# A fused convolution and feed-forward kernel: block 0 of x loaded by POOL ahead of the weights, first weight quarter cast by ScalarE

## The chip, the core and the metric

The kernel runs on one core of one Trainium2 chip. Its engines work side by side, each with an instruction queue of its own: TensorE (PE, with weight loads shown as PEld), VectorE (DVE), ScalarE (ACT), GpSimd (POOL) and SyncE (SP). They meet through semaphores. DMA transfers are issued from the queues of SP, ACT and POOL and carried by 16 DMA engines. A transfer that changes the type (fp32 in DRAM to bf16 on chip) is issued by POOL in this kernel. SBUF has 128 partitions; PSUM takes the matmul results.

The metric is the device time of one execution in microseconds, the median of the runs.

## The reference, cut to what matters

```python
# x (8, 3904, 192), weight (8, 7); moe_w1, moe_w2 (192, 1024); moe_w3 (1024, 1024); moe_w_out (1024, 192)
w = softmax(weight, axis=-1)                     # 7 taps for each of 8 heads of 24 channels
x_pad = concat([zeros(B, 6, 192), x], axis=1)    # each sequence starts with zeros
attn[b, s, h, g] = sum_k w[h, k] * x_pad[b, s + k, h, g]
t = attn.reshape(31232, 192)
out = ((t @ w1) * (t @ w2) @ w3) @ w_out         # (31232, 192), fp32
```

The second line of matrices is linear after the product, so the kernel computes W = w3 @ w_out once, and then `(a * b) @ W`.

## The kernel before, in words

The 31232 tokens are cut into two halves of 15616 tokens, `r = 0` and `r = 1`. Half 0 stands on partitions 0 to 63 and half 1 on 64 to 127 wherever 64 rows of a contraction are enough, so that two matmuls with 64 rows each run on the array together. The weights `w1` and `w2` are the tiles `wd[0]` and `wd[1]`, `[128, 3, 1024]` in bf16; each holds its weight twice, once on each half of the partitions.

**Convolution.** A window is 64 rows of x, of which 58 give outputs. A block is a number of windows (`SIZES` is 10, 8, 10, 34, ...), loaded as `xb`. For each head a 64x64 band matrix in `Aband` holds the 7 taps, and a matmul (line 271) of band and window gives the convolved rows, which are moved to `convo`. The bands are made in four steps of `band(g, e, f)`: VectorE multiplies taps and diagonals (line 230, `cprod`), TensorE sums 14 matmuls (line 236), and the engine `f` moves the result to `Aband` (line 238). For the first blocks TensorE transposes `convo` (line 324) and the result is moved to `xT`; later blocks are stored to DRAM (`rows`, line 315) and come back by transposing DMAs (line 344).

**First product.** `first_product(R)` goes through 8 feature blocks of 128 columns (`ft`) for 512 tokens of each half. For each `ft` there are 12 matmuls for `w1` and 12 for `w2` (line 371, written together as `wd`), ScalarE copies the one result (line 377, `asb`), and VectorE multiplies it with the other (line 378, `abT`). `between` puts other work after the feature block with the given number. PSUM is given out as four pairs of banks in rotation.

**Second product.** `second_product` (line 397) multiplies `abT` with `W_sb`, ScalarE moves the result (line 402), and a DMA stores it. W itself is made once after the first three rounds: TensorE transposes w3 (line 433) and multiplies it with w_out (line 443).

**The order.** It is written out by hand: instructions stand in each engine's queue in the order of the program. Within the prologue it is this:

- SP loads block 0 of x in fp32 into `x32`, which takes a buffer of the `abT` ring: six transfers (lines 153 to 158).
- POOL makes `diag` (two `affine_select`, line 169), then copies two values of `x32` into `pace`, so that its queue waits for x (line 173), and then issues the weight loads, which cast to bf16 (line 166). They come in quarters of 256 columns (`WC`): quarter 0 of `wd[0]` and `wd[1]` to partitions 0 to 63, quarter 0 of `wd[0]` once more to partitions 64 to 127, and then quarters 1, 2 and 3 of both to partitions 0 to 63.
- SP copies what is missing on partitions 64 to 127 from partitions 0 to 63 by DMA, seven transfers (`copy_w`, line 350).
- ScalarE casts the first half of block 0 (line 201) and three windows of the second (line 462); VectorE casts the last two (line 467) and zeroes the six rows ahead of the sequence's start in half 1 (line 465).
- TensorE runs four matmuls on zeros, the broadcast of the taps, two more on zeros (line 187, `warm`), the bands, the convolution and the transposes of block 0, and then `first_product(0)`. The convolution of block 1 stands after its feature block 5, with the second half's results moved by VectorE, and its transposes after feature block 6.
- After the weights POOL issues the loads of blocks 1 and 2, then w_out, the eight row blocks of w3, and blocks 3 and 4 (`load_wo`, `load_w3`, `load_x`).

Of the kernel before, what the change touches and what calls it, by code (L numbers as in the profile page):

```python
# [8 lines left out]
FP32 = mybir.dt.float32  # L9
# [7 lines left out]
def kernel(  # L17
# [39 lines left out]
    def tok(i):  # L57
        return (i // WB) * S + (i % WB) * ST
# [3 lines left out]
    work = ctx.enter_context(tc.tile_pool(name="work", bufs=2))  # L62
# [8 lines left out]
    def banks():  # L71
        p = free.pop(0)
        return p, pairs[:, NS * p:NS * p + NS, :]
# [14 lines left out]
    def halves_of(b):  # L88
        n = SIZES[b] // 2
        return [(FIRST[b], 2 * n)] if 2 * n <= MAXN else [(FIRST[b], n), (FIRST[b] + n, n)]  # L90

    x_rows = x.rearrange("b s d -> (b s) d")
    xb_of, zero_rows = {}, {}

    def x_spans(r, i, m):
        return bass.AP(tensor=x.tensor, offset=(r * TS + tok(i) - PAD) * D,
                       ap=[[D, Q], [ST * D, m], [1, D]])

    def load_x(b, parts=(0, 1)):
        tiles = xb_of.setdefault(b, [])  # L100
        zeros_of = zero_rows.setdefault(b, [])
        for i0, n in [v for e, v in enumerate(halves_of(b)) if e in parts]:
            xb = work.tile([128, n, D], BF16, tag="xb", bufs=5, name="xb")
            w = 0
            while w < n:
                i = i0 + w
                m = min(n - w, WB - i % WB)
                at_end = i + m == NWIN
                if at_end:
                    m -= 1  # L110
                if m:
                    for r in range(NS):
                        nc.gpsimd.dma_start(out=xb[Q * r:Q * r + Q, w:w + m, :],  # L113
                                            in_=x_spans(r, i, m))
                if i % WB == 0:
                    zeros_of += [(xb, 0, w), (xb, 1, w)]
                w += m
                if at_end:
                    nc.gpsimd.memset(xb[Q:128, w, :], 0.0)
                    t = tok(NWIN - 1) - PAD  # L120
                    nc.gpsimd.dma_start(out=xb[0:Q, w, :], in_=x_rows[t:t + Q, :])
                    nc.gpsimd.dma_start(out=xb[Q:Q + PAD + LAST, w, :],
                                        in_=x_rows[TS + t:TS + t + PAD + LAST, :])
                    w += 1
            if len(halves_of(b)) == 1:
                tiles += [(xb, 0), (xb, SIZES[b] // 2)]
            else:
                tiles.append((xb, 0))
# [4 lines left out]
    n0 = SIZES[0] // 2  # L133
    xb0 = work.tile([128, 2 * n0, D], BF16, tag="xb", bufs=5, name="xb")
    xb_of[0] = [(xb0, 0), (xb0, n0)]
    x32 = work.tile([128, 2 * n0, D], FP32, tag="abT", bufs=GROUP, name="x32")
    pace = const.tile([1, 2], BF16)
    tiny = const.tile([128, 1], FP32)
    ones = const.tile([128, 1], BF16)
# [4 lines left out]
    nc.vector.memset(tiny, 0.0)  # L144
    nc.vector.memset(ones, 1.0)
    nc.vector.memset(zeros, 0.0)  # L146
    nc.vector.memset(x32[0:Q, 0, :], 0.0)
    nc.vector.memset(half, 0.0)
    nc.vector.memset(half[:, Q:2 * Q], 1.0)
    nc.vector.memset(identw, 0.0)  # L150
    nc.scalar.activation(out=tiny, in_=tiny, func=ACT.Exp)

    nc.sync.dma_start(out=x32[Q:128, 0:n0, :], in_=x_spans(1, 0, n0))
    nc.sync.dma_start(out=x32[0:Q, 1:n0, :], in_=x_spans(0, 1, n0 - 1))
    for s0, s1 in ((PAD, PAD + 48), (PAD + 48, Q)):
        nc.sync.dma_start(out=x32[s0:s1, 0, :], in_=x_rows[s0 - PAD:s1 - PAD, :])
    for r in range(NS):
        nc.sync.dma_start(out=x32[Q * r:Q * r + Q, n0:, :], in_=x_spans(r, n0, n0))

    WC = (0, DFF // 4, DFF // 2, DFF * 3 // 4, DFF)  # L160
    wd = [const.tile([128, NP, DFF], BF16, name=f"wd{i}", tag=f"wd{i}") for i in range(2)]
    w_rows = [w.rearrange("(k q) f -> q k f", q=Q) for w in (moe_w1, moe_w2)]

    def load_w(part, i, r=0):
        cs = slice(WC[part], WC[part + 1])
        nc.gpsimd.dma_start(out=wd[i][Q * r:Q * r + Q, :, cs], in_=w_rows[i][:, :, cs])  # L166

    for p0 in (0, Q):
        nc.gpsimd.affine_select(
            out=diag[p0:p0 + Q], in_=ones[p0:p0 + Q].to_broadcast([Q, Q + PAD]),  # L170
            pattern=[[-1, Q + PAD]], compare_op=ALU.is_equal, fill=0.0, base=0,
            channel_multiplier=1)
    nc.gpsimd.tensor_copy(out=pace, in_=x32[0:1, n0 - 1, 0:2])
    load_w(0, 0)
    load_w(0, 1)
    load_w(0, 0, 1)
    for part in range(1, len(WC) - 1):
        for i in range(2):
            load_w(part, i)
    ident, swapped = identw[:, 0:128], identw[:, Q:Q + 128]  # L180

    def warm(n, t=None):
        p = None
        if t is None:
            p, t = banks()
# [12 lines left out]
    nc.vector.tensor_tensor(  # L198
        out=wall, in0=wall, in1=wmax.unsqueeze(2).to_broadcast([1, H, K]), op=ALU.subtract)
    nc.scalar.activation(out=wall, in_=wall, func=ACT.Exp)  # L200
    nc.scalar.copy(out=xb0[:, 0:n0, :], in_=x32[:, 0:n0, :])
    nc.vector.tensor_copy(out=identw[0:Q, 0:Q], in_=diag[0:Q, 0:Q])
    nc.vector.tensor_copy(out=identw[0:Q, 128:128 + Q], in_=diag[0:Q, 0:Q])
    nc.vector.reduce_sum(out=wsum, in_=wall, axis=AX.X)
# [2 lines left out]
        out=wrow, in0=wall, in1=wsum.unsqueeze(2).to_broadcast([1, H, K]), op=ALU.mult)  # L207
# [20 lines left out]
    def band(g, e, f):  # L228
        c = slot([128, K, Q], BF16, "cprod")
        nc.vector.tensor_tensor(  # L230
            out=c, in0=taps, in1=wsb[:, g, e].unsqueeze(2).to_broadcast([128, K, Q]),
            op=ALU.mult)
        p, bps = banks()
        for v, lhsT in enumerate((ident, swapped)):
            for k in range(K):
                nc.tensor.matmul(bps[:, 0, v * Q:v * Q + Q], lhsT, c[:, k, :],
                                 start=(k == 0), stop=(k == K - 1))
        f(out=Aband[:, g, e].rearrange("p v s -> p (v s)"), in_=bps[:, 0, 0:2 * Q])
        drained(p)
# [78 lines left out]
    def pe_transpose(b, k):  # L318
        n = SIZES[b] // 2
        convo = convo_of[b]  # L320
        p, tps = banks()
        tps = bf16(tps)
        for w in range(n):
            nc.tensor.transpose(
                out=tps[:, w, :],
                in_=convo[:, w, k].rearrange("p r g -> p (r g)"), identity=ident)
# [21 lines left out]
    def copy_w(part, i, f):  # L348
        cs = slice(WC[part], WC[part + 1])
        f(out=wd[i][Q:128, :, cs], in_=wd[i][0:Q, :, cs])  # L350
# [70 lines left out]
    def load_wo():  # L421
        nc.gpsimd.dma_start(out=wo_b, in_=wor)
# [26 lines left out]
    V, A, P = nc.vector.tensor_copy, nc.scalar.copy, nc.gpsimd.tensor_copy  # L449

    def move(f, pair):
        f(out=pair[0], in_=pair[1])

    copy_w(0, 1, nc.sync.dma_start)
    for part in range(1, len(WC) - 1):
        for i in range(2):
            copy_w(part, i, nc.sync.dma_start)
    load_x(1)
    load_x(2)

    band(0, 0, A)
    A(out=xb0[:, n0:n0 + 3, :], in_=x32[:, n0:n0 + 3, :])
    band(0, 1, A)
    band(1, 0, A)
    nc.vector.memset(xb0[Q:Q + PAD, 0, :], 0.0)
    band(1, 1, A)
    V(out=xb0[:, n0 + 3:, :], in_=x32[:, n0 + 3:, :])
    for h, f in ((0, V), (2, A), (4, V), (6, A)):
        p, moves = conv(0, h, 2, ())
        for m in moves:  # L470
# [2 lines left out]
    for k, f in ((0, V), (1, A), (2, V)):  # L473
        p, *m = pe_transpose(0, k)
        move(f, m)
        drained(p)
    load_wo()
    for jt in range(JT):
        load_w3(jt)
# [3 lines left out]
    def seq(*fs):  # L483
        def run():
            for f, *a in fs:
                f(*a)
        return run

    first_product(0, {
        5: seq((conv, 1, 0, 4), (conv, 1, 4, 4, (V,))),  # L490
        6: seq((pe_transposes, 1))})
    first_product(1, {
        0: seq((conv, 2, 0, 4)),
# [80 lines left out]
```

## Time and profile before

| what | value |
|---|---|
| median of 3 runs | 531.38 us (530.8 to 532.62) |
| the profiled execution's own time | 532.29 us |
| its span on the core | 530.5 us |
| mean granted TensorE clock | 0.993 |
| TensorE busy | 519.4 us, 98% of the span |
| VectorE, ScalarE busy | 361.8 us (68%), 325.6 us (61%) |
| POOL busy | 55.5 us (10%) |
| share of the chain that ended last | TensorE 86% |

The span is the time from the first to the last instruction of the profiled execution; its own time, measured from outside, is 1.79 us longer. Rows of the timeline begin with start and duration in microseconds; in brackets stands how long the engine was idle before, and what ended that. Rows of groups end with busy time and mean duration in ns, and after the second bar with the idle time before them. Rows that begin with two times and a colon are stretches of the span: for each engine the busy time and the number of instructions, then the granted clock, the DMA engines' share and GB/s.

### The profile page before, as it was taken

Reading aid. Unit: us, or ns where it says so; the run is one execution under the profiler, and the core shown is the slowest. Engines: PE = TensorE matmul, PEld = TensorE weight load, DVE = VectorE, ACT = ScalarE, POOL = GpSimd, SP = SyncE. Lnnn points to the kernel's source line nnn. Section 1 sums busy time; section 2 is a strip of 40 time slices with the busy share of each in tenths; the row PEclk is TensorE's granted clock in tenths of the full one; section 3 lists DMA queues with packets and bytes.
Section 4 is the critical chain, followed back from the end, with each engine's and each line's share of the span. In section 5 each row is a group of like instructions: output and inputs, shape, how many; then the busy total and the mean of one; then the engine's idle time right before and its main releaser. Section 6 shows DMA issues by size and latency. Waiting matters only on the chain.

```text
span 530.5 us, 12833 instructions
## 1 busy us (share of the span) xinstructions
PE 519.4 (98%) x5482; PEld 346.1 (65%) x5482; DVE 361.8 (68%) x349; ACT 325.6 (61%) x410; POOL 55.5 (10%) x95
## 2 busy tenths in 40 slices
PE   6899999999999999999999999999999999999997
PEld 4345786557955579555894558845588555995587
DVE  5478664996559964699537994389943999038940
ACT  4488726775367743777437774377733777357752
POOL 6451024110002100021000200012000000000000
PEclk9799999999999999999999999999999999999999
DMA  7999299992478933788356964569445411430014
GB/s 128 198 201 190 38 205 188 184 144 66 147 178 119 111 90 124 177 117 107 90 151 160 123 90 114 147 153 120 62 120 161 118 32 31 135 122 1 1 61 150
DMA packets 128749, 64.39 MB, mean 121 GB/s; under 512 B 82168, under 2 KB 126839, under 8 KB 128691
## 3 DMA queue, kind: packets, MB, share of 16 engines
q1 hardware_dynamic: 89153, 43.29, 32.9%
q0 software_dynamic: 39392, 20.18, 29.3%
q8 instruction: 43, 0.70, 0.6%
q14 instruction: 15, 0.12, 0.1%
q10 hardware_dynamic: 146, 0.10, 0.1%
HBM read 33.45 MB, written 34.82 MB: 129 GB/s over the span
## 4 chain that ended last, share of the span: by engine, by line
PE 86%; DVE 1%; ACT 0%; issue 0%; POOL 0%; ACTq 0%; POOLq 0%
PE pairs L371 53%; PE pairs L397 31%; PE pairs L271 2%; DVE abT L378 1%; PE pairs L443 1%; ACT asb L377 0%; PE pairs L433 0%; ACT osb L402 0%; POOL pace L532 0%; ACTq L402 0%; POOLq L532 0%
## 5 line engine op out<-in xcount | busy, mean ns | idle before, releaser
L378 DVE TENSOR_TENSOR abT<-asb,pairs 128x1024 bf16<-128x1024 bf16 (+1 forms) x248 | 298.3, 1204 | 85.6 <-ACT asb L377 40.3
L371 PE MATMUL pairs<-xT,wd 64*128 64x512 bf16 (+1 forms) x2976 | 322.7, 375 | 3.9 <-DMA wd<-wd 2.8
L377 ACT CAST asb<-pairs 128x1024 bf16<-128x1024 f32 (+1 forms) x248 | 247.6, 998 | 75.7 <-PE pairs L371 75.3
L371 PEld LDWEIGHTS <-wd 64*128 64x128 bf16 x2976 | 164.8, 94 | 157.3 <-issue 7.5
L397 PEld LDWEIGHTS <-abT 128*128 128x128 bf16 x1952 | 159.8, 98 | 9.0 <-issue 9.0
L397 PE MATMUL pairs<-W_sb,abT 128*128 128x192 bf16 x1952 | 165.6, 246 | 0.0
L402 ACT COPY osb<-pairs 128x384 f32<-128x384 f32 x122 | 58.3, 478 | 117.0 <-PE pairs L397 117.0
L288 DVE CAST convo<-pairs 128x864 bf16<-128x864 f32 (+8 forms) x67 | 52.6, 840 | 56.6 <-PE pairs L271 56.6
L113 POOL DMA_DIRECT2D xb<-in_x_dram x38 | 30.1, 801 | 10.3 <-PE pairs L371 3.4
L532 POOL COPY pace<-abT 1x2 bf16<-1x2 bf16 x10 | 1.8, 177 | 251.7 <-DVE abT L378 251.7
L271 PE MATMUL pairs<-xb,Aband 64*64 64x432 bf16 (+4 forms) x320 | 16.7, 307 | 0.5 <-DVE abT L378 0.2
L402 DVE COPY osb<-pairs 128x192 f32<-128x192 f32 x1 | 0.4, 358 | 16.4 <-PE pairs L397 16.4
L271 PEld LDWEIGHTS <-Aband 64*64 64x64 bf16 x320 | 6.5, 105 | 6.0 <-issue 4.1
L409 POOL DMA_DIRECT2D out_dram<-osb x6 | 4.6, 771 | 25.5 <-ACT osb L402 25.5
L288 ACT CAST convo<-pairs 128x816 bf16<-128x816 f32 (+6 forms) x11 | 6.3, 614 | 1.0 <-PE pairs L271 1.0
L443 PE MATMUL pairs<-wo_b,w3T 128*128 128x192 bf16 x64 | 6.3, 246 | 0.1
L443 PEld LDWEIGHTS <-w3T 128*128 128x128 bf16 x64 | 5.2, 97 | 1.5 <-issue 1.5
L166 POOL DMA_DIRECT2D wd<-in_moe_w_dram x9 | 5.8, 653 | 0.0
L426 POOL DMA_DIRECT2D w3b<-in_moe_w_dram x8 | 4.3, 552 | 6.2 <-DMA xb<-in_x_dram 5.3
L433 PE MATMUL pairs<-identw,w3b 128*128 128x128 bf16 x64 | 4.6, 219 | 0.0
L436 DVE COPY w3T<-pairs 128x1024 bf16<-128x1024 bf16 x4 | 2.8, 690 | 2.4 <-ACT W_sb L445 1.4
L187 PE MATMUL pairs<-zeros 128*128 128x512 bf16 x6 | 2.9, 625 | 1.3 <-DVE zeros L146 1.3
(54 smaller groups left out, 49.0 us busy)
## 6 DMA issues: line engine op xcount, KB each, us to landing
out_dram<-osb SPq DMA_DIRECT2D x54, 384.0 KB, 3.6
xb<-in_x_dram POOLq DMA_DIRECT2D x14, 432.0 KB, 7.4
rows<-convo SPq DMA_DIRECT2D x6, 648.0 KB, 7.9
out_dram<-osb POOLq DMA_DIRECT2D x6, 384.0 KB, 9.3
w3b<-in_moe_w_dram POOLq DMA_DIRECT2D x8, 256.0 KB, 11.4
xb<-in_x_dram POOLq DMA_DIRECT2D x4, 408.0 KB, 12.9
xb<-in_x_dram POOLq DMA_DIRECT2D x4, 384.0 KB, 6.6
xT<-rows SPq DMA_TRANSPOSE x84, 3.0
```

Of the source, the lines that this page charges most:

```text
L113: nc.gpsimd.dma_start(out=xb[Q * r:Q * r + Q, w:w + m, :], in_=x_spans(r, i, m))
L166: nc.gpsimd.dma_start(out=wd[i][Q * r:Q * r + Q, :, cs], in_=w_rows[i][:, :, cs])
L271: nc.tensor.matmul(view(slice(Q * c, Q * c + Q), r)[:, :, j * G:(j + 1) * G], band_of(h, r), xb[Q * r:Q * r + Q, w0:w0 + n, h * G:(h + 1) ...
L288: f[e % len(f)](out=dst, in_=part)
L371: nc.tensor.matmul(p[:, r, 0:N], wd[i][rs, k, ft * 128:(ft + 1) * 128], xT[k][rs, r0:r0 + N], start=(k == 0), stop=(k == NP - 1))
L377: nc.scalar.copy(out=asb[:, :, 0:N], in_=pa[:, :, 0:N])
L378: nc.vector.tensor_tensor(out=ab[:, ft, :, 0:N], in0=asb[:, :, 0:N], in1=pb[:, :, 0:N], op=ALU.mult)
L397: nc.tensor.matmul(ops[:, (g - g0) * D:(g - g0) * D + D], ab[:, jt, r, g * 128:(g + 1) * 128], W_sb[:, jt, :], start=(jt == 0), stop=(jt = ...
L402: f(out=osb[:, g0:g0 + per, :].rearrange("p g d -> p (g d)"), in_=ops[:, 0:per * D])
L409: queue.dma_start(out=out[t0:t0 + ng * 128, :].rearrange("(g p) d -> p g d", p=128), in_=osb)
L433: nc.tensor.transpose(out=tps[:, gt, :], in_=w3b[:, gt * 128:(gt + 1) * 128], identity=ident)
L443: nc.tensor.matmul(wps[:, 0, 0:D], w3T[:, gt, :], wo_b[:, gt, :], start=(gt == 0), stop=(gt == JT - 1))
```

## The change

Block 0 of x no longer passes through fp32 on chip: POOL loads it into `xb0` with the cast in the DMA, in four transfers (nine windows for each half, and the 58 rows of the first window for each half), of which the first stands ahead of the `affine_select`s; there is no `pace` copy any more in the prologue. The rows ahead of the sequences' starts are zeroed by VectorE at the start. SP loads quarter 0 of both weights as fp32 into `wfirst`, and ScalarE casts each to both halves (`cast_w`). The other quarters are loaded by POOL, quarter 3 behind block 1 of x, and copied to partitions 64 to 127 by VectorE (quarter 1) and POOL (quarters 2 and 3). The last band is moved by VectorE; two matmuls on zeros stand behind the bands. Half of block 1's convolution moves from feature block 5 to 3, and ScalarE moves all its results.

```diff
-    x32 = work.tile([128, 2 * n0, D], FP32, tag="abT", bufs=GROUP, name="x32")
+    wfirst = work.tile([Q, 2, NP, DFF // 4], FP32, tag="abT", bufs=GROUP, name="wfirst")
...
-    nc.vector.memset(x32[0:Q, 0, :], 0.0)
+    nc.vector.memset(xb0[:, 0, :], 0.0)
...
-    nc.sync.dma_start(out=x32[Q:128, 0:n0, :], in_=x_spans(1, 0, n0))
-    nc.sync.dma_start(out=x32[0:Q, 1:n0, :], in_=x_spans(0, 1, n0 - 1))
-    for s0, s1 in ((PAD, PAD + 48), (PAD + 48, Q)):
-        nc.sync.dma_start(out=x32[s0:s1, 0, :], in_=x_rows[s0 - PAD:s1 - PAD, :])
-    for r in range(NS):
-        nc.sync.dma_start(out=x32[Q * r:Q * r + Q, n0:, :], in_=x_spans(r, n0, n0))
...
+    for i in range(2):
+        nc.sync.dma_start(out=wfirst[:, i], in_=w_rows[i][:, :, 0:WC[1]])
+
+    def load_w(part):
         cs = slice(WC[part], WC[part + 1])
-        nc.gpsimd.dma_start(out=wd[i][Q * r:Q * r + Q, :, cs], in_=w_rows[i][:, :, cs])
-
+        for i in range(2):
+            nc.gpsimd.dma_start(out=wd[i][0:Q, :, cs], in_=w_rows[i][:, :, cs])
+
+    def load_x0(r):
+        nc.gpsimd.dma_start(out=xb0[Q * r:Q * r + Q, 1:, :], in_=x_spans(r, 1, 2 * n0 - 1))
+
+    load_x0(0)
     for p0 in (0, Q):
         nc.gpsimd.affine_select(
...
-    nc.gpsimd.tensor_copy(out=pace, in_=x32[0:1, n0 - 1, 0:2])
-    load_w(0, 0)
-    load_w(0, 1)
-    load_w(0, 0, 1)
-    for part in range(1, len(WC) - 1):
-        for i in range(2):
-            load_w(part, i)
+    load_x0(1)
+    for r in range(NS):
+        nc.gpsimd.dma_start(out=xb0[Q * r + PAD:Q * r + Q, 0, :],
+                            in_=x_rows[r * TS:r * TS + ST, :])
+    load_w(1)
+    load_w(2)
+    load_x(1)
+    load_w(3)
+    load_x(2)
...
-    nc.scalar.copy(out=xb0[:, 0:n0, :], in_=x32[:, 0:n0, :])
...
-    copy_w(0, 1, nc.sync.dma_start)
-    for part in range(1, len(WC) - 1):
-        for i in range(2):
-            copy_w(part, i, nc.sync.dma_start)
-    load_x(1)
-    load_x(2)
-
+    def cast_w(i, r):
+        A(out=wd[i][Q * r:Q * r + Q, :, 0:WC[1]], in_=wfirst[:, i])
+
+    cast_w(0, 0)
+    cast_w(0, 1)
+    cast_w(1, 0)
     band(0, 0, A)
-    A(out=xb0[:, n0:n0 + 3, :], in_=x32[:, n0:n0 + 3, :])
     band(0, 1, A)
     band(1, 0, A)
-    nc.vector.memset(xb0[Q:Q + PAD, 0, :], 0.0)
-    band(1, 1, A)
-    V(out=xb0[:, n0 + 3:, :], in_=x32[:, n0 + 3:, :])
+    band(1, 1, V)
+    cast_w(1, 1)
+    warm(2)
...
+    for part, f in ((1, V), (2, P), (3, P)):
+        for i in range(2):
+            copy_w(part, i, f)
     load_wo()
...
     first_product(0, {
-        5: seq((conv, 1, 0, 4), (conv, 1, 4, 4, (V,))),
+        3: seq((conv, 1, 0, 4)),
+        5: seq((conv, 1, 4, 4)),
         6: seq((pe_transposes, 1))})
```

`V`, `A` and `P` are the copies of VectorE, ScalarE and POOL.

More of the change, by code (lines that the diff above doesn't have):

```diff
@@ L162 @@
     w_rows = [w.rearrange("(k q) f -> q k f", q=Q) for w in (moe_w1, moe_w2)]
-    def load_w(part, i, r=0):
+    for i in range(2):
+        nc.sync.dma_start(out=wfirst[:, i], in_=w_rows[i][:, :, 0:WC[1]])
+    def load_w(part):
         cs = slice(WC[part], WC[part + 1])
-        nc.gpsimd.dma_start(out=wd[i][Q * r:Q * r + Q, :, cs], in_=w_rows[i][:, :, cs])
+        for i in range(2):
[3 more added lines that the diff above has]
+    load_x0(0)
     for p0 in (0, Q):
```

## The prediction

> **What bounds the kernel now.** I read the page first, then the timeline of the first 16 us, then stretches of 2 us with the granted clock, then the waits. The page:
>
> ```profile
> span 530.5 us, 12833 instructions
> PE 519.4 (98%) x5482; PEld 346.1 (65%) x5482; DVE 361.8 (68%) x349; ACT 325.6 (61%) x410; POOL 55.5 (10%) x95
> L371 PE MATMUL pairs<-xT,wd 64*128 64x512 bf16 (+1 forms) x2976 | 322.7, 375 | 3.9 <-DMA wd<-wd 2.8
> ```
>
> TensorE is busy for 98% of the span. Line 371, the first product, is idle 3.9 us in 2976 matmuls, and 2.8 of that is one wait for a copy of the weights inside SBUF. So nearly everything after the prologue is TensorE's own work, and a microsecond taken from its start comes off the end. The timeline of TensorE shows where the wait lies:
>
> ```profile
> 8.28 0.57 PE L236 MATMUL pairs<-cprod,identw 128*128 128x64 bf16 x14 [0.99 <-DVE cprod L230]
> 8.78 1.03 PE L271 MATMUL pairs<-xb,Aband 64*64 64x120 bf16 x32
> 10.21 1.12 PE L324 MATMUL pairs<-identw,convo 128*128 128x128 bf16 x15 [0.40 <-ACT convo L452]
> 11.26 1.32 PE L371 MATMUL pairs<-xT,wd 64*128 64x512 bf16 x7
> 15.42 1.04 PE L371 MATMUL pairs<-xT,wd 64*128 64x512 bf16 x4 [2.84 <-DMA wd<-wd]
> ```
>
> The product starts at 11.26, stops after 7 matmuls and goes on at 15.42. It also goes on slowly. In the next rows (stretches of 2 us; then stretches with line 371 alone) the figure behind the busy times is the granted clock:
>
> ```profile
> 14.00:16.00 2.00, 0.58 (x4) 0.29 (x6) 0.00 (x0) 0.00 (x0) 2.00 (x3) 0.65 1.33 188
> 20.00:22.00 2.00, 2.00 (x14) 0.78 (x12) 0.89 (x2) 1.01 (x1) 0.03 (x1) 0.65 1.36 213
> 15.40:21.40 6.00, 5.98 (x30) 2.16 (x32) 0.50 1.41 195
> 21.40:25.40 4.00, 4.00 (x39) 1.79 (x35) 1.00 1.43 205
> ```
>
> From 15.4 to 21.4 the clock is 0.50: 30 matmuls in 6 us, then 39 in 4. A mean of 0.65 in 14 to 16 and again in 20 to 22 puts the half clock from about 14.6 to 21.4. Half of the 6.0 us that were worked in it, 3.0 us, is lost. So the late weights cost 2.84 in waiting and 3.0 in clock, 5.84 us.
>
> Why they are late:
>
> ```profile
> 5.96 0.18 POOL L173 CAST pace<-x 1x2 bf16<-1x2 f32 x1 [4.36 <-DMA x<-in_x_dram]
> 6.08 5.81 POOL L166 DMA_DIRECT2D wd<-in_moe_w_dram  x9
> 10.06 7.24 SPq L350 DMA_DIRECT2D wd<-wd  x7
> SPq L350 <- DMA wd<-in_moe_w_dram: 7.1, 3, 5.4
> DMA to landing us min/median/max: 6.7/6.7/6.7
> ```
>
> POOL holds the weights back until x has landed (5.96), then issues nine transfers. SP waits for one to land before it can copy it to the other half (10.06), and that copy of `wd[1]`, in a queue full of other weights, takes 6.7 us (last row, line 350): the chain x, weights, copy is serial.
>
> **The change part by part.**
>
> *First quarter of weights.* SP issues two fp32 loads at once in place of six x loads; ScalarE casts each to both halves, four casts of 64x768. The copy by DMA and its 6.7 us are gone. Rows for the casts and for the loads:
>
> ```profile
> 0.82 0.76 SPq L153 DMA_DIRECT2D x<-in_x_dram  x1
> L201 ACT CAST xb<-x 128x960 bf16<-128x960 f32 x1 | 1.0, 992 | 3.4 <-DMA x<-in_x_dram 3.4
> L462 ACT CAST xb<-x 128x576 bf16<-128x576 f32 x1 | 0.7, 674 | 0.7 <-DMA x<-in_x_dram 0.7
> 0.00:2.00 2.00, 0.67 (x2) 0.28 (x3) 0.89 (x7) 0.64 (x1) 0.69 (x6) 1.00 0.00 0
> 4.00:6.00 2.00, 2.00 (x24) 1.27 (x24) 1.87 (x4) 0.00 (x0) 0.04 (x1) 1.00 0.89 196
> 8.00:10.00 2.00, 1.53 (x46) 1.12 (x45) 1.18 (x4) 1.65 (x6) 2.00 (x4) 1.00 1.08 133
> ```
>
> From 992 and 674 ns, a cast costs 0.83 ns an element and 0.19 us: 0.83 us for 768, 3.3 us for four. The two ScalarE casts of x, 1.67 us, go away. The weights are 2 x 196 KB; at 196 GB/s (the row of 4 to 6 us, fp32 loads) they take 2.0 us alone. SP's first issue stands at 0.82 and nothing moves before 2 us (0 GB/s in the row of 0 to 2); from about 2.2, shared with x, they land at about 4.5 and 5.5. ScalarE then casts from 4.5: three done at about 7.0, three band evictions of 0.27 until 7.8, the fourth at 8.6. The product needs it at 11. Cost on the path: nothing, with 2.4 us of cover; beyond that, microsecond for microsecond.
>
> *x of block 0.* Two transfers of nine windows and two of single rows, now by POOL with the cast in the DMA, two `affine_select`s between them. Rows:
>
> ```profile
> 1.06 0.54 POOL L169 TENSOR_SCALAR_AFFINE_SELECT diag<-ones 64x70 bf16<-64x70 bf16 x2 [0.53 <-DVE ones L145]
> L113 POOL DMA_DIRECT2D xb<-in_x_dram x38 | 30.1, 801 | 10.3 <-PE pairs L371 3.4 <-DMA w3b<-in_moe_w_dram 3.2 <-DMA xb<-in_x_dram 2.8
> L121 POOL DMA_DIRECT2D xb<-in_x_dram x1 | 0.6, 561 | 0.0
> 8.29 0.67 ACT L462 CAST xb<-x 128x576 bf16<-128x576 f32 x1 [0.75 <-DMA x<-in_x_dram]
> DMA  9999999899997963200000005479999978899899
> 2.46 0.16 DVE L202 COPY identw<-diag 64x64 bf16<-64x64 bf16 x1
> ```
>
> POOL issues from about 0.8: 0.80 + 0.54 + 0.80 + 2 x 0.56, all out by 4.1. Data: 0.49 MB as bf16 at 133 (cast loads, 8 to 10 us) to 196 GB/s is 2.5 to 3.7 us, and the first weights 2.0 beside it, so 4.5 to 5.7 us from 2.2: the last packet at 6.7 to 7.9, and 0.9 to land: the row of digits is the DMA engines' busy share from 6 to 9 us in 40 slices, and x's last packets end in its 19th, at 7.4, where ScalarE is released at 8.29. I take 8.0. Bounds: 6.8 if the two streams overlap fully; 10.3 if x takes what the fp32 x took (8.29) and the weights' 2.0 come on top. `diag` moves from 1.6 to about 2.2; VectorE copies it at 2.46 today, so that is covered by 0.3 us, and costs what it exceeds.
>
> The Trainium skill ("DMA: Bandwidth & Descriptors", Why a DMA increments its semaphore by 16 and not by 1) has the number of engines of a transfer as the largest divisor up to 16 of its slowest dimension, with an exception for some transfers by GpSimd: 58 rows would go over 2 engines, and this stands against the new row loads. No run here shows it; the sum doesn't use it.
>
> *Bands.* Today VectorE's zeroing waits for ScalarE's cast of x, and holds up the fourth product:
>
> ```profile
> 4.21 1.70 DVE L230 TENSOR_TENSOR cprod<-diag,wsb 128x448 bf16<-128x448 bf16 x3
> 4.89 2.40 PE L236 MATMUL pairs<-cprod,identw 128*128 128x64 bf16 x42
> 7.45 0.14 DVE L465 MEMSET xb<- 6x96 uint32 x1 [1.54 <-ACT xb L201]
> 7.60 0.62 DVE L230 TENSOR_TENSOR cprod<-diag,wsb 128x448 bf16<-128x448 bf16 x1
> L238 ACT CAST Aband<-pairs 128x128 bf16<-128x128 f32 x4 | 0.9, 266 | 0.0
> ```
>
> The zeroing moves to the start, so the fourth product follows at 5.9 and its matmuls run on from 7.29 to about 7.9 (0.57 to 0.8 us). Two added warming matmuls wait for a bank that ScalarE drains behind its casts, at about 7.3; they take 0.4 to 1.0, to 8.4 to 8.9. The convolution starts at about 8.5 (today 8.78), bound below by 8.2, above by x at 10.3. From there to the product it is 11.26 - 8.78 = 2.48, so the product starts at 11.0: 0.3 us gained, between 0.6 gained and 1.6 lost.
>
> *The other quarters.* SP's remaining copies go to VectorE (quarter 1) and POOL (2 and 3). One feature block of the product takes 2.60 us (41.62 / 16):
>
> ```profile
> 83.95 41.62 PE L371 MATMUL pairs<-xT,wd 64*128 64x512 bf16 x384
> L378 DVE TENSOR_TENSOR abT<-asb,pairs 128x1024 bf16<-128x1024 bf16 x24 | 29.3, 1221 | 12.8 <-PE pairs L371 7.6 <-ACT asb L377 3.9
> L377 ACT CAST asb<-pairs 128x1024 bf16<-128x1024 f32 x24 | 24.3, 1014 | 13.0 <-PE pairs L371 13.0
> L452 DVE COPY xT<-pairs 128x580 bf16<-128x580 bf16 x2 | 0.9, 460 | 0.2 <-PE pairs L324 0.2
> L119 POOL MEMSET xb<- 64x192 bf16 x1 | 0.3, 258 | 0.0
> 53.79 1.54 PE L433 MATMUL pairs<-identw,w3b 128*128 128x128 bf16 x24
> ```
>
> So the quarters are needed at 11.0, 16.2, 21.8 (with a convolution half between) and 27.5. POOL issues quarter 1 by 5.4 and quarter 2 by 6.7; with x ahead in the queue they land at about 9.5 and 11. VectorE's two copies (460 ns for 580 elements, so at most 0.6 each) come at about 11.8, ahead of its first multiplication, which waits for matmuls until 13.6: covered. POOL's copies have no row; the nearest is a 64x192 memset of 258 ns, so 0.26 to 1.03 us for four times the elements; I take 1.0, and four of them, done by about 16 once quarter 3 has landed at 14. That is 5 us or more ahead of need. POOL then issues w_out and the w3 rows at about 16, not 14.67, into emptier DMA engines (0.67 MB of copies are gone); w3 is first used at 53.79 today, about 48 afterwards. Nothing.
>
> *Convolution of block 1* starts at feature block 3, with evictions by ScalarE alone. Its x is issued by 8 and needed at 21. Zero to 0.3; I take 0.1, since ScalarE's own copy of a block takes 1.01 of each 2.60 us there.
>
> *Sum.* 2.84 + 3.0 + 0.3 - 0.1 = 6.0 off 530.5: span 524.5. The profiled execution took 532.29, 1.79 more than its span, and 0.91 more than the median 531.38. Against the median: 525.4.
>
> **The rivals.**
>
> *The clock stays at half for a while* (the wait goes, part of its clock loss doesn't). The prologue works TensorE in patches, with gaps of 0.40 and 0.99 us today; if such a stretch counts as idle, the product begins at 0.50. For it: the granted clock fell at 14.6 after only 2 us of full idleness. Against: with the same gaps it was 1.00 in the row of 8 to 10. Price: half of a slow stretch half as long as today's 6.8, 1.7 us: 527.1. The Trainium skill ("TensorE: Matmul & The Clock Gate", What's actually happening) has free-running windows of 3.41 us, one idle window throttling the clock; the trace agrees, as its 6.8 us are two of them, and by that rule the phase of the windows decides this rival.
>
> *x is late* (the other side). Four transfers of POOL carry the cast, and everything waits for the last of them. From a landing near 10.5, TensorE idles 2 us after the bands, as it did before 14.6, and the clock falls: the delay of 2.0, plus up to 3.4: 525.4 + 5.4 = 530.8, no gain. Each microsecond more adds one; at 12.7 it is slower than before by over 0.3%. Against: that is 4.4 us later than the fp32 x landed.
>
> *Later quarters are late.* If a POOL copy took over 4.5 us (VectorE holding it up), block 4 would wait. 2 us late gives 527.5, and 530.5 with the clock. Against: its nearest row is 0.26 us, and 5 us of slack stand ahead.
>
> *The change does not do what it says*: the wait reappears at block 0 for the casts, if the fp32 weights land after 7.5 instead of 5.5. That gives 526 to 528. Against: they are first in SP's queue.
>
> **How the numbers follow.** Forecast (wait and slow clock both gone) 0.64, 524.0 to 526.8 by the bounds of the terms; half clock for a window 0.12; x late 0.13 (0.03 faster, 0.05 same, 0.05 slower); quarters late 0.05 (0.03 faster, 0.01 same, 0.01 slower); casts late 0.06. Faster 0.88, same 0.06, slower 0.06; 0.3%, 1.6 us, is about what this measurement tells from no change (530.8 to 532.62). The range, 523.6 to 529.0, holds the first two, the casts and part of the others.
>
> **What would show it.** Right: no wait of line 371 for DMA in the first 30 us; clock 1.00 from 8 us on; product started near 11.0 and first group done by 48; four casts at ScalarE ended by 9. Wrong: the convolution waiting for a DMA past 10; a granted clock of 0.50 after 11; line 371 waiting for ScalarE's or POOL's copies.

## The result and the profile after

| | before | after |
|---|---|---|
| median, us | 531.35 (530.8 to 532.62, 4 runs) | 525.65 (525.07 to 525.99, 4 runs) |
| profiled execution, us | 532.29 | 525.64 |
| its span, us | 530.5 | 523.9 |
| mean granted clock | 0.993 | 1.000 |

The ratio is 0.9888, 95% interval 0.9869 to 0.9908: 5.7 us less. In the page of the changed kernel the two lines that answer to those of before:

```profile
span 523.9 us, 12818 instructions
PE 516.8 (99%) x5484; PEld 344.1 (66%) x5484; DVE 362.5 (69%) x348; ACT 327.7 (63%) x413; POOL 59.4 (11%) x99
L373 PE MATMUL pairs<-xT,wd 64*128 64x512 bf16 (+1 forms) x2976 | 319.6, 373 | 0.6 <-ACT xT L338 0.2
```

The first product (now line 373) is idle for 0.6 us in place of 3.9, and none of it is a wait for a DMA. Its busy time is 3.1 us less for the same matmuls, which is the clock. TensorE's timeline of the prologue:

```profile
4.89 3.15 PE L238 MATMUL pairs<-cprod,identw 128*128 128x64 bf16 x56
8.00 0.84 PE L190 MATMUL pairs<-zeros 128*128 128x512 bf16 x2
8.76 0.61 PE L273 MATMUL pairs<-xb,Aband 64*64 64x120 bf16 x32
11.04 5.83 PE L373 MATMUL pairs<-xT,wd 64*128 64x512 bf16 x48
47.48 1.53 PE L435 MATMUL pairs<-identw,w3b 128*128 128x128 bf16 x24
```

The four bands run on without a gap, the convolution starts at 8.76 (8.78 before), the product at 11.04 (11.26), and it runs 48 matmuls without a pause where it stopped after 7. The transposes of w3 start at 47.48 in place of 53.79: 6.3 of the 6.6 us are gained by then. In stretches of 2 us the clock is full, in 14 to 16 and 20 to 22 too, where it was 0.65:

```profile
10.00:12.00 2.00, 1.87 (x22) 1.25 (x24) 1.75 (x5) 0.95 (x2) 1.96 (x4) 1.00 1.34 145
14.00:16.00 2.00, 2.00 (x20) 0.96 (x18) 1.99 (x3) 1.52 (x2) 0.82 (x1) 1.00 1.52 184
20.00:22.00 2.00, 2.00 (x35) 1.10 (x34) 1.47 (x2) 2.00 (x4) 1.66 (x4) 1.00 1.50 203
```

And what the new steps cost on ScalarE, POOL and VectorE (timeline):

```profile
4.34 1.67 ACT L457 CAST wd<-wfirst 64x768 bf16<-64x768 f32 x2 [1.34 <-DMA wfirst<-in_moe_w_dram]
6.95 0.83 ACT L457 CAST wd<-wfirst 64x768 bf16<-64x768 f32 x1 [0.94 <-DMA wfirst<-in_moe_w_dram]
8.29 0.83 ACT L457 CAST wd<-wfirst 64x768 bf16<-64x768 f32 x1
1.33 0.91 POOL L166 DMA_DIRECT2D xb<-in_x_dram  x1 [0.80 <-POOLq L562]
11.52 1.65 POOL L352 COPY wd<-wd 64x768 bf16<-64x768 bf16 x2
11.64 1.81 DVE L352 COPY wd<-wd 64x768 bf16<-64x768 bf16 x2
16.24 0.82 POOL L352 COPY wd<-wd 64x768 bf16<-64x768 bf16 x1 [0.92 <-DMA wd<-in_moe_w_dram]
```

The casts take 0.83 us each and end at 9.1, 1.9 us ahead of the product. The last of POOL's copies ends at 17.1.

How long a feature block takes decides when each copy is needed. ScalarE copies one result of each feature block as soon as its matmuls are done, and in the changed kernel these copies stand 1.29 us apart:

```profile
12.21 1.01 ACT L379 CAST asb<-pairs 128x1024 bf16<-128x1024 f32 x1 [0.69 <-PE pairs L373]
13.50 1.01 ACT L379 CAST asb<-pairs 128x1024 bf16<-128x1024 f32 x1 [0.28 <-PE pairs L373]
14.79 1.01 ACT L379 CAST asb<-pairs 128x1024 bf16<-128x1024 f32 x1 [0.28 <-PE pairs L373]
```

A feature block is 12 matmuls, 6 for each weight (three tiles, two halves), and not 12 for each weight, as the description of the kernel before says. The 384 matmuls in 41.62 us that the prediction shows are therefore 32 feature blocks of 1.30 us, where it reckoned with 16 of 2.60. The 48 matmuls from 11.04 on are four feature blocks. Quarter 1 of the weights is needed with the third of them, at about 14.1 (14.79 less the 0.65 us of six matmuls), and VectorE's copies of it end at 13.45.

### The profile page after: what moved, and what is told of

Same layout as the page of the kernel before. It is cut to its first block, busy times and chain, and to the rows that moved or that the text cites. A ratio compares the mean times of both kernels' runs of the same rounds, so it can differ in the third digit from the quotient of the medians.

```text
span 523.9 us, 12818 instructions
## 1 busy us (share of the span) xinstructions
PE 516.8 (99%) x5484; PEld 344.1 (66%) x5484; DVE 362.5 (69%) x348; ACT 327.7 (63%) x413; POOL 59.4 (11%) x99
## 4 chain that ended last, share of the span: by engine, by line
PE 88%; DVE 0%; ACT 0%; issue 0%; ACTq 0%
PE pairs L373 54%; PE pairs L399 31%; PE pairs L273 2%; PE pairs L445 1%; DVE abT L380 0%; PE pairs L435 0%; ACT osb L404 0%; ACTq L404 0%
## 5 line engine op out<-in xcount | busy, mean ns | idle before, releaser
L373 PEld LDWEIGHTS <-wd 64*128 64x128 bf16 x2976 | 162.6, 94 | 152.7 <-issue 3.1
L290 DVE CAST convo<-pairs 128x864 bf16<-128x864 f32 (+7 forms) x65 | 51.6, 849 | 56.6 <-PE pairs L273 56.6
L457 ACT CAST wd<-wfirst 64x768 bf16<-64x768 f32 x4 | 3.3, 831 | 2.3 <-DMA wfirst<-in_moe_w_dram 2.3
```

The source lines that it names most:

```text
L290: f[e % len(f)](out=dst, in_=part)
L373: nc.tensor.matmul(p[:, r, 0:N], wd[i][rs, k, ft * 128:(ft + 1) * 128], xT[k][rs, r0:r0 + N], start=(k == 0), stop=(k == NP - 1))
```

## The experiments

There are two questions: which part of the change carries the 5.7 us, and whether the sum's two terms, 2.84 us of waiting and 3.0 us of slow clock, are what they were taken for. Each median stands beside the median of the kernel before on the same chip.

| run | what | us | kernel before | ratio, 95% interval |
|---|---|---|---|---|
| e2 | before, with the change's weights alone | 529.77 | 530.73 | 0.9979, 0.9966 to 0.9992 |
| e3 | before, with its x alone | 530.17 | 530.73 | 0.9987, 0.9972 to 1.0003 |
| e11 | before, with its copies alone | 527.62 | 530.57 | 0.9941, 0.9915 to 0.9966 |
| e4 | changed, the copies by SP | 527.29 | 530.73 | 0.9932, 0.9911 to 0.9952 |
| e9 | changed, quarter 1's copy by SP | 527.74 | 532.13 | 0.9929, 0.9905 to 0.9953 |
| a2 | changed | 525.80 | 532.13 | 0.9903, 0.9876 to 0.9930 |
| e6 | changed, without the two matmuls on zeros | 525.68 | 532.13 | 0.9884, 0.9864 to 0.9905 |
| e8 | changed, casts later | 525.91 | 532.13 | 0.9893, 0.9875 to 0.9911 |
| e5 | changed, x behind quarters 1 and 2 | 529.62 | 530.82 | 0.9977, 0.9956 to 0.9998 |
| e1 | before, filler ahead of the product | 530.58 | 530.73 | 0.9994, 0.9977 to 1.0011 |
| e10 | before, filler inside the wait | 530.82 | 530.82 | 0.9992, 0.9977 to 1.0008 |
| e12 | e11 with that filler | 528.72 | 530.57 | 0.9962, 0.9945 to 0.9979 |

### The three parts alone

**The weights alone.** x stays fp32 on SP, behind the first quarter:

```diff
+    for i in range(2):
+        nc.sync.dma_start(out=wfirst[:, i], in_=w_rows[i][:, :, 0:DFF // 4])
     nc.sync.dma_start(out=x32[Q:128, 0:n0, :], in_=x_spans(1, 0, n0))
...
-    load_w(0, 0)
-    load_w(0, 1)
-    load_w(0, 0, 1)
...
-    copy_w(0, 1, nc.sync.dma_start)
...
+    for r in range(NS):
+        nc.scalar.copy(out=wd[0][Q * r:Q * r + Q, :, 0:WC[1]], in_=wfirst[:, 0])
     nc.scalar.copy(out=xb0[:, 0:n0, :], in_=x32[:, 0:n0, :])
...
+    cast_w(1, 0)
     band(0, 0, A)
...
     band(1, 1, A)
+    cast_w(1, 1)
```

> The kernel before, with the change's weights alone: the first quarter as fp32 by SP ahead of x and cast by ScalarE to both halves; x still in fp32 by SP behind it, the other quarters behind x by POOL and copied by SP. Theory: line 371 waits for no DMA at its start, but x comes 2 us later (2 x 196 KB at 196 GB/s) and so does the convolution, about 10.8; the product starts at about 13.3. 5.84 - 2.0 = 3.8 us gained, 527.5, if the clock holds, and up to 3.4 less, 531, if TensorE's idle stretch ahead of the convolution brings it down. Rival (the weights are all of the gain and x's route is worth nothing): 525.6.

```profile
10.03 0.57 PE L238 MATMUL pairs<-cprod,identw 128*128 128x64 bf16 x14 [2.75 <-DVE cprod L232]
10.53 1.28 PE L273 MATMUL pairs<-xb,Aband 64*64 64x120 bf16 x32
14.22 9.70 PE L373 MATMUL pairs<-xT,wd 64*128 64x512 bf16 x72
12.00:14.00 2.00, 1.50 (x15) 1.50 (x15) 0.98 (x3) 1.43 (x5) 2.00 (x4) 0.50 1.14 145
```

The timeline has no wait for the weights any more, but x comes later, VectorE's zeroing behind ScalarE's cast of x holds back the fourth band for 2.75 us, and in this execution the clock fell at once (0.50 in the stretch of 12 to 14). The product starts at 14.22. One microsecond is gained. Nine of the ten executions had the clock full or nearly so and took 528.86 to 530.06, where the expectation for a clock that holds was 527.5. What those executions waited for no trace shows; quarter 1 still came by SP's copies, which at half clock, as here, nothing waits for.

**x alone.** The four transfers of POOL stand ahead of the weights, as in the change, and SP's loads of x and the casts go; the nine weight loads and SP's seven copies are as before:

```diff
+    load_x0(0)
     for p0 in (0, Q):
...
-    nc.gpsimd.tensor_copy(out=pace, in_=x32[0:1, n0 - 1, 0:2])
+    load_x0(1)
+    for r in range(NS):
+        nc.gpsimd.dma_start(out=xb0[Q * r + PAD:Q * r + Q, 0, :],
+                            in_=x_rows[r * TS:r * TS + ST, :])
     load_w(0, 0)
```

> The kernel before, with the change's x alone: block 0 by POOL with the cast in the DMA, ahead of all weights; the weights then by POOL in nine transfers and copied by SP as before. Theory: the convolution starts at 8.3 to 8.8, the serial chain of load and copy of the first quarter stays, about 1 us earlier (issued at 4.7 in place of 6.08), so the product still waits 1.5 to 2.8 us for a copy of the weights and the clock still falls: 529.5 to 531.4. Rival (x's route and its smaller load are what gains): 525.6 to 526.5.

```profile
8.01 0.69 PE L270 MATMUL pairs<-xb,Aband 64*64 64x120 bf16 x32 [0.19 <-DMA xb<-in_x_dram]
10.35 1.32 PE L370 MATMUL pairs<-xT,wd 64*128 64x512 bf16 x7
15.14 9.13 PE L370 MATMUL pairs<-xT,wd 64*128 64x512 bf16 x56 [3.46 <-DMA wd<-wd]
```

The product starts 0.9 us earlier and waits 0.6 us longer: its second weight is there at 15.14, at 15.42 before. The gain of 0.6 us lies within the interval.

**The copies alone.** Quarters 1 to 3 copied by VectorE and POOL; x, quarter 0 and its one copy by SP as before:

```diff
     copy_w(0, 1, nc.sync.dma_start)
-    for part in range(1, len(WC) - 1):
-        for i in range(2):
-            copy_w(part, i, nc.sync.dma_start)
...
+    for part, f in ((1, V), (2, P), (3, P)):
+        for i in range(2):
+            copy_w(part, i, f)
     load_wo()
```

> The kernel before, with the change's copies alone: quarters 1 to 3 copied to partitions 64 to 127 by VectorE and POOL instead of six of SP's seven DMAs; x, quarter 0 and its one copy by SP as before. Theory as it now stands (three serial things end close together, quarter 0's copy, quarter 1's copy and x, and taking one away uncovers the next): the copy of the second weight's quarter 0 is still issued at 10.1 and behind POOL's loads in the queues, so the product waits until 14 to 15.4 and the clock falls; quarter 1 is no longer late, but at half clock nothing waits for it. 530 to 531. Rival (the six copies were what made the first one late): the wait goes nearly, 526 to 528.

```profile
11.68 1.89 PE L371 MATMUL pairs<-xT,wd 64*128 64x512 bf16 x7
14.81 7.29 PE L371 MATMUL pairs<-xT,wd 64*128 64x512 bf16 x65 [1.25 <-DMA wd<-wd]
10.00:12.00 2.00, 1.87 (x17) 1.47 (x19) 1.28 (x4) 1.17 (x3) 2.00 (x4) 0.62 1.21 150
12.00:14.00 2.00, 1.57 (x7) 0.45 (x4) 1.25 (x3) 0.81 (x1) 2.00 (x4) 0.52 1.03 146
14.00:16.00 2.00, 1.19 (x12) 0.60 (x14) 0.26 (x1) 0.20 (x1) 1.96 (x3) 1.00 1.29 151
```

The expectation was wrong: the theory missed, and the rival's band holds the number but not by its mechanism. This part, which the prediction costed at nothing, brings 2.95 us alone, the most of the three. The copy of quarter 0 lands only 0.6 us earlier (14.81), so the six copies had not made it late; but behind it the product runs 65 matmuls without a pause, at full clock. The clock was at half ahead of that: means of 0.62 and 0.52 put it from about 10.5 to 13.9, over the transposes and the first seven matmuls. It cost nothing here, since TensorE then waited for the copy in any case.

### Waiting and clock

**A filler ahead of the product.** Twelve matmuls on zeros, before `first_product(0)`, in the kernel before:

```diff
+    warm(12)
     first_product(0, {
```

> The kernel before, with twelve more matmuls on zeros ahead of the first product (2.6 us at full clock), in the time in which TensorE waits anyway. Theory (the late copy costs 2.84 us of waiting and 3.0 us of clock, and the two are separate terms): the second weight's copy still lands at about 15.4, so the wait's end doesn't move, but the clock stays at 1.00 through 14 to 22 us; 3.0 us are gained, 528.4, and w3's transposes start at about 50.8 in place of 53.79. Rival (the slow clock has another cause than the idle stretch): half clock from 14.6 as before, 531.4.

```profile
11.80 3.46 PE L187 MATMUL pairs<-zeros 128*128 128x512 bf16 x11 [0.22 <-issue]
21.61 2.11 PE L371 MATMUL pairs<-xT,wd 64*128 64x512 bf16 x17 [0.19 <-DMA wd<-wd]
12.00:14.00 2.00, 2.00 (x6) 0.69 (x5) 0.07 (x1) 0.00 (x0) 2.00 (x4) 0.58 1.11 162
```

It gained nothing (530.58). In its profile the clock was near half when the filler began (0.58 from 12 to 14), so eleven recorded matmuls took 3.46 us and pushed the product to 15.19; the expectation had reckoned with full clock there. From about 13.7 on the clock was full, and the product waited for a copy only 0.19 us, at 21.61. This execution's span is 528.6, 1.9 us below that of the profiled execution before, and yet the median is that of the kernel before. So the execution that the 3.0 us were read from was one of the slower ones, and most lose less to the clock.

**A filler inside the wait**, between the first and the second weight's matmuls, pushes nothing back:

```diff
                             start=(k == 0), stop=(k == NP - 1))
+                if R == 0 and ft == 0 and i == 0:
+                    warm(12)
```

> The kernel before, with twelve matmuls on zeros between the first and the second weight's matmuls of the first feature block, so inside the wait for the copy; nothing else is pushed back (2.6 us at full clock, 5.1 at half, into a wait of 2.8). Theory (waiting and slow clock are separate terms, and idleness in the wait brings the clock down): the wait shrinks to the filler plus a rest, the product still goes on at about 15.4, the clock stays at 1.00 behind it: 528 where the clock was full at 12, a median of 528 to 529. Rival 1 (the clock's fall doesn't come from that idle stretch): half clock for 6.8 us as before, 530.7 or more, since the filler then ends behind the wait. Rival 2 (the patchy stretch ahead of the product brings the clock down in many executions, before the wait): runs spread between 528 and 531.

```profile
12.65 2.76 PE L187 MATMUL pairs<-zeros 128*128 128x512 bf16 x12
15.35 2.98 PE L371 MATMUL pairs<-xT,wd 64*128 64x512 bf16 x25
20.16 4.70 PE L371 MATMUL pairs<-xT,wd 64*128 64x512 bf16 x41 [1.84 <-DMA wd<-wd]
14.00:16.00 2.00, 2.00 (x13) 0.76 (x13) 0.00 (x0) 0.00 (x0) 1.85 (x3) 1.00 1.37 192
```

Here the clock is 1.00, and the median is that of the kernel before, not the 528 to 529 expected. The product goes on at 15.35 at full speed and stops at 18.33, after 25 matmuls: six of the first feature block, twelve of the second, and of the third the first weight's six and one more. There it waits 1.84 us for the second weight's quarter 1, which lands at 20.16. So the slow clock had been hiding a second late copy: in this execution, 1.84 of the 3.0 us booked for the clock. The size differs between executions, as the 0.19 us of the run before this one shows.

The kernel before's own executions say the same. Of 70 on four chips, with a median of 530.9 us, the 18 with a mean granted clock of 1.000 have a median of 530.4, the 13 with 0.990 to 0.994 one of 532.5. So the clock is worth some 2 us where it falls for long, and 0.5 in the middle of the executions, and the other 4.8 us from 530.4 down to 525.65 are there without it.

**The same filler with the copies by the engines:**

> The run before this one, with twelve matmuls on zeros inside the wait, between the first and the second weight's matmuls of the first feature block. With SP's copies the same filler held the clock at 1.00 in its profile, and the product then waited 1.8 us for quarter 1. Theory (the slow clock hid a late quarter 1; with both gone the 3.0 us of clock come out): no wait for quarter 1, clock 1.00 from the product on, 527.5 to 528.5 where the clock was full when the filler began. Rival (the clock's 3.0 us can't be had by holding the clock): as with SP's copies, 530 to 531.

```profile
14.77 7.80 PE L371 MATMUL pairs<-xT,wd 64*128 64x512 bf16 x66
16.00:18.00 2.00, 2.00 (x22) 0.92 (x20) 1.39 (x2) 1.01 (x1) 2.00 (x3) 1.00 1.56 186
```

There is no wait for quarter 1 and the clock is 1.00; the median is 528.72, 0.2 above the expected band and 2.1 below the run with the same filler and SP's copies, each against nearly the same time of the kernel before. So the copies gain with the filler too. The filler itself adds nothing to them: without it the same program took 527.62, and the intervals of the two overlap. The theory, that the clock's 3.0 us would come out once quarter 1 was no longer late, did not hold.

### Undoing parts of the change

**All six copies by SP again.**

```diff
-    for part, f in ((1, V), (2, P), (3, P)):
-        for i in range(2):
-            copy_w(part, i, f)
+    for part in range(1, len(WC) - 1):
+        for i in range(2):
+            copy_w(part, i, nc.sync.dma_start)
```

> The changed kernel with the other quarters copied to partitions 64 to 127 by SP's DMAs as before, in place of VectorE's and POOL's copies. Theory (only the first quarter is on the path; the others have 4 us or more of slack, and the DMA copies of 96 KB are late by at most 6.7 us): quarter 1 lands at 9.3 and its copy at 13 to 16, needed at 16.2; 525.6, with up to 1 us more if that copy is late. Rival (the copies by the engines carry part of the gain): a wait of line 371 for a DMA at about 16, 527 to 530.

```profile
11.01 3.27 PE L373 MATMUL pairs<-xT,wd 64*128 64x512 bf16 x25
15.38 2.76 PE L373 MATMUL pairs<-xT,wd 64*128 64x512 bf16 x23 [1.10 <-DMA wd<-wd]
```

**Quarter 1's copy by SP alone**, and the changed kernel beside it:

```diff
-    for part, f in ((1, V), (2, P), (3, P)):
+    for part, f in ((1, nc.sync.dma_start), (2, P), (3, P)):
```

> The changed kernel as it is, beside the next three on the same chip, as their measure. Some 5.7 us below the kernel before.

> The changed kernel with quarter 1 alone copied to partitions 64 to 127 by SP's DMAs; quarters 2 and 3 by POOL as changed. Theory (the wait of 1.1 us that the run with all copies by SP showed at 15.4 is quarter 1's, whose data lands only 7 us ahead of need and whose DMA copy takes 5 to 7 us behind the loads in the queues): a wait of 0.5 to 1.1 us at about 16 stays, 0.5 to 1.5 us above the changed kernel. Rival (all six DMA copies together slow the queues, and it is their number that makes them late): no wait, the changed kernel's time within 0.3.

```profile
PE pairs L373 <- DMA wd<-wd: 0.6, 2, 0.4
```

The rival of the first run is the one that held: with SP's copies the product waits 1.10 us at 15.38, and 2.3 of the 5.7 us are missing (527.29, on a chip whose kernel before was 0.6 us faster). With quarter 1 alone by SP the wait is 0.6 in two pieces and the span 525.0 against 524.0, and the median is 1.9 us over the changed kernel's, more than the 0.5 to 1.5 expected. The executions spread from 526.41 to 530.04 in the one and from 525.23 to 529.93 in the other, and the two intervals overlap, so the medians alone don't settle it. The traces do show the place: in both runs the product stops after 25 matmuls, one matmul into the third feature block, so the copy that is late is quarter 1's, by 0.2 to 1.1 us at a stop, even with all else changed. In the first run that stop lies at 14.28, not at the 16.2 that its expectation took from the prediction.

**x later.** Quarters 1 and 2 are issued ahead of x in POOL's queue:

```diff
-    load_x0(0)
     for p0 in (0, Q):
...
+    load_w(1)
+    load_w(2)
+    load_x0(0)
     load_x0(1)
...
-    load_w(1)
-    load_w(2)
     load_x(1)
```

> The changed kernel with quarters 1 and 2 of the weights issued ahead of block 0 of x in POOL's queue, so x is issued 2.6 us later. Theory (everything in the prologue waits for x): x lands at about 10.8, the convolution starts there and the product at 13.1; TensorE idles about 2 us after the bands and the clock falls for 3.4 to 6.8 us as it did ahead of 14.6 in the kernel before and at 11.0 in the run with the weights alone: 2.3 us of delay and 1.7 to 3.4 of clock, 529.6 to 531.3, close to the kernel before. Rival (the clock holds): 527.9. Rival (x's place in the queue doesn't matter, for x is released late by something else): 525.6.

```profile
11.63 1.11 PE L273 MATMUL pairs<-xb,Aband 64*64 64x120 bf16 x32 [3.04 <-DMA xb<-in_x_dram]
14.75 6.41 PE L373 MATMUL pairs<-xT,wd 64*128 64x512 bf16 x48
12.00:14.00 2.00, 1.67 (x41) 1.48 (x33) 1.50 (x4) 1.08 (x3) 1.89 (x3) 0.50 1.51 189
```

TensorE idles 3.04 us for x, the clock falls to 0.50, and 4.5 of the gain are gone, at the low end of the expected band. x's place ahead of the weights in the queue is needed.

**Without the two matmuls on zeros**, and **with the second weight's casts later**:

```diff
-    warm(2)
     for h, f in ((0, V), (2, A), (4, V), (6, A)):
```

> The changed kernel without the two matmuls on zeros behind the bands. Theory (they stand between the landing of x, about 8.2, and the convolution's start at 8.76, and the clock does not need them): the convolution starts at 8.2 to 8.3, 0.4 to 0.5 us below the changed kernel. Rival (they hold the clock: without them TensorE's patchy stretch from 8 to 11 us counts as idle): half clock for 3.4 us or more after 10 us, 1.7 to 3.4 us above the changed kernel, in some executions at least, which would show as a wider spread of the runs.

```diff
-    cast_w(1, 0)
     band(0, 0, A)
...
     band(1, 1, V)
-    cast_w(1, 1)
-    warm(2)
+    cast_w(1, 0)
     for h, f in ((0, V), (2, A), (4, V), (6, A)):
...
         drained(p)
+    cast_w(1, 1)
     for k, f in ((0, V), (1, A), (2, V)):
```

> The changed kernel without those two matmuls, and with ScalarE's two casts of the second weight behind the band evictions (the last of them behind the convolution's evictions) in place of one ahead of the bands and one behind. Theory: the bands no longer wait for the second weight's landing (6.9), x alone (8.2) releases the convolution; the second weight's casts are needed 1.3 us after the product's start and are done by then. Product start at about 10.5, 0.5 us below the changed kernel; no more than the run without the two matmuls gains, as x is the later one. Rival: the casts now stand ahead of the transposes' eviction by ScalarE, and cost as much as they save: 0.0 to 0.5 above the run without the two matmuls.

TensorE's timeline of the first of the two, at both ends of the kernel:

```profile
8.27 0.69 PE L273 MATMUL pairs<-xb,Aband 64*64 64x120 bf16 x32 [0.61 <-DMA xb<-in_x_dram]
10.61 5.66 PE L373 MATMUL pairs<-xT,wd 64*128 64x512 bf16 x48
468.00 2.19 PE L373 MATMUL pairs<-xT,wd 64*128 64x256 bf16 x36 [0.23 <-DVE abT L380]
```

The convolution starts at 8.27, released by x, and the product at 10.61, as expected and 0.6 us ahead of the changed kernel beside it (11.22). But the spans are 523.8 and 524.0, and the medians 525.68 and 525.80, which the intervals don't tell apart. The lead lasts to 464 us; there the last round, with blocks half as wide, waits 0.23 us for VectorE, which the changed kernel's trace doesn't show, and the lead shrinks to 0.2. Why the last round waits in the one and not in the other was not settled. The later casts (525.91) bring nothing either: their product starts at 10.41, and then pauses for ScalarE's move of `xT`, which stands behind a cast, as the rival had it.

```profile
10.41 0.39 PE L373 MATMUL pairs<-xT,wd 64*128 64x512 bf16 x2
11.24 5.14 PE L373 MATMUL pairs<-xT,wd 64*128 64x512 bf16 x46 [0.45 <-ACT xT L454]
```

No executions with a slower clock showed up without the two matmuls; with four executions that is weak. Neither version beats the changed kernel by more than the measurement can tell.

## Why the prediction was right, and where it wasn't

The median was forecast at 525.4 and came out at 525.65. That it came so close is luck in part: the clock's term was too large, the other quarters' too small, and the two made up for each other. By its own steps:

- **Wait of 2.84 us for quarter 0's copy.** Right: it is gone. The 6.7 us beside it are not that copy's: issued at 10.06 or later, it ended the wait at 15.42, so it took 5.4 us at most, and 6.7 is another's of the seven.
- **Clock, 3.0 us.** This is the term that was mis-sized. It was read from one execution at 0.993 and worked out as if TensorE, at full clock, could have used all of that time. The filler inside the wait shows that it could not: in its profile, at full clock, the product waited 1.84 us for quarter 1. The prediction asked what is late next of the changed kernel only, and not what the slow clock was hiding in the kernel before. Over executions the clock is worth less still: the kernel before takes 530.4 where it stays full, 530.9 over all.
- **When each quarter is needed.** Wrong by a factor of two, as a feature block takes 1.30 us and not 2.60. In the changed kernel quarter 1 is needed at about 14.1, not 16.2, quarter 2 at 17.1, not 21.8, and quarter 3 at 20.3, not 27.5 (17.11 and 20.30 are the next starts of the product in its timeline, behind the two halves of block 1's convolution). The "5 us or more ahead of need" were 3.9 and 3.2 for POOL's copies, and VectorE's came about 1.3 us ahead. The same slip hides the late copy of the kernel before: at full clock from 15.42, the second weight of the third feature block comes up at about 17.9 with 1.30 us a block, and only at about 21 with 2.60, when the copy would long have been there (20.16 in the filler's run). Both figures are estimates from these rows.
- **The other quarters, "covered", nothing.** For the changed kernel this was right. As the cost of a part it was wrong: these copies alone are worth 2.95 us, and without them the changed kernel gives 2 us back. The sum came out right because microseconds of theirs stood in the clock's term.
- **x at 8.0, between 6.8 and 10.3.** The convolution started at 8.27 in the run without the two matmuls on zeros, where x released it. In the prediction's row of digits the busy stretch ends in the 17th slice, at 7.28, not in the 19th, so the 0.9 us to landing are 1.0. POOL began its first transfer at 1.33, not 0.8. The two row loads, which by the Trainium skill ("DMA: Bandwidth & Descriptors", Why a DMA increments its semaphore by 16 and not by 1) could have gone over 2 engines only, took 4.0 and 4.4 us from issue to landing, behind x transfers of 5.0 and 5.5; no slow tail is seen, so they fall under the page's exception or the tail was hidden.
- **Bands to 7.9, convolution at 8.5, product at 11.0.** 8.04, 8.76 and 11.04: the 0.3 us were 0.2.
- **Casts.** 0.83 us each, as worked out; the second weight landed at 6.9, not 5.5, and the last cast ended at 9.1, not 8.6. The cover held.
- **POOL's copies** took 0.82 us (1.0 taken). **VectorE's** took 0.9 us each, not 0.6. Its first multiplication, which the prediction put at 13.6, could have started at 13.22, when ScalarE's copy was done, and started at 13.48 behind the copies; TensorE did not wait for it.
- **Rivals.** The late x did not come true, but its mechanism was shown when it was forced: 3.0 us of idling and half clock. Half clock at the product's start was seen in no profile of the changed kernel, though two of six executions on one chip took 528.0 and 529.93, the second with a mean clock of 0.996; no trace shows what those two lost or where, so whether this rival came true in them stays open.

What the parts bring alone, 1.0, 0.6 and 2.95 us, is 4.5 in sum, and together they bring 5.7. The difference lies within the intervals of the four ratios. That each part alone stops at the next late thing is shown for x (which waits for quarter 0's copy) and, with the clock held, for quarter 0 (which is followed by the wait for quarter 1); that this makes up the missing 1.2 us is not shown. The move of block 1's convolution and of the last band to another engine were not tried alone.

## What to carry to other kernels

A slow stretch behind a stall is not a loss of its own until it is known what would have been ready at full speed: list the next loads with their landing times, and book only what is left after them. For that list, count the matmuls of a block in the code and check its length against a row, such as the distance of two copies of its results. When several serial loads end close together ahead of the same work, moving one of them brings little, and the parts have to be tried together and one by one. A copy of 96 KB through the DMA queues took 5 to 7 us behind other loads where an engine did it in under one; whether that matters depends on the slack, and here some 5 us of it were not enough: SP issued quarter 1's copy at 9.17, and the product stood still for it at 14.28.

## What the runs showed of the hardware

VectorE's copies of 64x768 took 418 and 659 ns in the run with the copies alone, where POOL copied nothing at that time, and 903 and 980 ns in the changed kernel, where POOL's copies ran beside them:

```profile
L350 DVE COPY wd<-wd x2: 418/538/659, 12.3 to 12.6; 64x768 bf16<-64x768 bf16 x2
L352 DVE COPY wd<-wd x2: 903/942/980, 11.6 to 12.5; 64x768 bf16<-64x768 bf16 x2
L352 POOL COPY wd<-wd x4: 819/824/877, 11.5 to 16.2; 64x768 bf16<-64x768 bf16 x4
```

(In each row the shortest, median and longest in ns, and the first and last start.) The Trainium skill ("SBUF — State Buffer", Who interferes with whom) has the two engines share one pair of ports, which a VectorE copy can use too, and whoever comes first holds it for a whole instruction. The trace agrees: POOL's copies started first, at 11.52, and took 0.82 to 0.88 us as elsewhere (0.82 in the other run), VectorE's are the ones that grew, and the last of them ends 0.28 us after POOL's (13.45 and 13.17 us).

The granted clock fell in stretches of 3.4 and 6.8 us that began at another place in each profile: at 14.6 in the kernel before, 11.0 with the weights alone, 10.1 with x late, and 10.5 with the copies alone. These times are worked out from the mean clock of stretches of 2 us, with a clock of 0.50 inside: for the copies alone, 0.62 and 0.52 are 1.52 and 1.92 us at half clock, together 3.44, which end at 13.9. The same program had a mean clock of 1.000 in some executions and of 0.99 in others.
